# Key-value and row products of four tiles in quarters of the array, 64 by 64

## The chip, the core and the metric

One core of one Trainium2 chip. The metric is the time of the whole kernel on the device, in microseconds. The engines are named as the profile names them: PE (TensorE, matmuls; its weight loads are the row PEld), DVE (VectorE), ACT (ScalarE), POOL (GpSimd) and SP (SyncE, which here issues DMAs).

## What is computed

Attention without a softmax on 8 batches, 8 heads, 576 rows and 64 columns, each head's output divided by the root of its mean square, and a two-layer network behind it:

```python
kv  = einsum('bhsd,bhse->bhde', k, v)          # 64 x 64 for each head
out = einsum('bhsd,bhde->bhse', q, kv)
x   = out / sqrt(mean(out * out, -1) + 1e-6) * g_norm    # -> 4608 rows x 512
h   = x @ w_in                                  # 512 -> 2048
y   = (h / (1 + exp(-1.702 * h))) @ w_out       # 2048 -> 512
```

Inputs and result are float32; the matmuls take float16 and add up in float32.

## The kernel before

There are nine tiles, t = 0 to 8. Tiles 0 to 7 hold the first 512 rows of one batch each, tile 8 the last 64 rows of all eight. While PE runs the network of tile t, the attention of batch b = t + 1 is made in between, and the key-value product of batch t + 2. The order is written by hand: each engine executes its instructions in the order in which the program issues them, and two dictionaries, `u1` for the first layer and `u2` for the second, say after which step a piece of other work is issued. `at2(i, f)` puts `f` behind matmul i of the second layer.

From tile 1 on each layer is done with seven half-size products instead of eight (a scheme with sums of quarters). In the first layer (`SevenIn`, `hid_seven`) the steps stand in a plan such as `LATER`, two digits for a group of columns and a product; the matmuls are those of L589. In the second layer (`Seven.run`) the products come in the order 1, 5, 6, 2, 7, 3, 4 with 16 matmuls each (L709, 128 x 256), so matmuls 0 to 15 are product 1, 16 to 31 product 5, 80 to 95 product 3. Products 5, 6, 7 and 3 take sums of the gated rows, the quarters 0 to 3 of `gS`, which VectorE forms (L641); `later` in the plan says when. In `LATER` the first half of quarter 3 is formed behind matmul 58, and two products of the first layer's last group ('34') are left for matmul 15.

PSUM has eight banks: three with the tag `att` (pool `ps_a`), three `hT` (`ps_h`), two `o` (`ps_o`). The tiles of a pool take its banks in turn, so a new tile waits for the readers of the third last one.

The attention of a batch b from 2 on, as far as the change touches it:

- `kv_products` (L264): for four pairs of heads, 5 x 2 matmuls (L248) with 128 rows of `k` as weights (64 columns, one head) and 64 columns of `v`. One head of the pair goes to the upper half of the PSUM partitions, the other to the lower. The fifth step is the rest, 64 rows, the other 64 being zero. All goes to one bank, `kvp`.
- `kv_copies` (L271, `keep_kv`): four copies of 64 x 256 from `kvp` to `kb` (the tile `kvd`), since each head's product is wanted on the upper and on the lower 64 partitions. On ScalarE, behind matmul 52.
- `rows` (L328): 2 x 16 matmuls (L337) with 64 rows of the transposed queries as weights (128 columns) and 64 columns of `kb`. The two row halves of the array (`half`) write to two banks.
- Then `squares` of the four banks on ScalarE (L347, `sq`), `add_up` on VectorE (L353, `sum`), `roots` on ScalarE (L362), `turn` on VectorE (L367, `x`), and a DMA that transposes `x` into `xT`, the input of the next tile. `xS` (L517) are sums of quarters of `xT`.

In `LATER`, `rows` is `(15, 15)`: behind matmul 15 of the second layer PE runs the key-value products of batch t + 2, and straight after them the rows of batch b.

Of the kernel before, what the change touches and what calls it, by code (L numbers as in the profile page):

```python
# [8 lines left out]
F32 = mybir.dt.float32  # L9
# [3 lines left out]
P = 128  # L13
# [3 lines left out]
def kernel(  # L17
# [203 lines left out]
    class Attention:  # L221
# [47 lines left out]
        def kv_products(self):  # L269
            self.kvp = ps_a.tile([P, NPAIR, D], F32, name="kvp", tag="att")  # L270
            for js in (range(J), (J,)):  # L271
                for c in range(NPAIR):
                    self.kv_product(self.kvp[:, c, :], c, js, c == 0)

        def kv_copies(self, engine):
            self.engine = engine
            self.keep_kv(0, NPAIR)
# [35 lines left out]
        def out(self, c):  # L313
# [11 lines left out]
            nc.scalar.activation(sq[:, 0:n], t, AFT.Square)  # L325
            self.o[c] = (t, sq, n)

        def rows(self, i):  # L328

            t = [  # L330
                pool.tile([P, DM], F32, name="outR", tag=tag)
                for pool, tag in ROW_BANKS[i]
            ]
            for h in range(H):
                for half in range(2):
                    r = slice(half * D, (half + 1) * D)
                    nc.tensor.matmul(  # L337
                        t[half][:, h * D : (h + 1) * D],
                        self.qTd[r, h * (J // 2) + i, :],
                        self.kb[r, h // 2, half, 1 - h % 2, :],  # L340
                        start=(h == 0),
                        stop=True,
                        skip_group_check=True,
                    )
            for half in range(2):
                sq = attn.tile([P, SM], F16, name="sq", tag="sq", bufs=4)
                nc.scalar.activation(sq, t[half], AFT.Square)  # L347
                self.o[2 * i + half] = (t[half], sq)
# [572 lines left out]
    for fo in COLS[0:GROUP]:  # L921
# [38 lines left out]
        "aahh",  # L960
        {15: '34'},
        (0, 0, 6, 11),
        {'rows': (15, 15), 'add_up': (17, 20, 24, 28), 'table': 24, 'roots': (28, 29), 'turn': (35, 38, 46, 48)},
    )
    LAST_TWO = Plan(
# [21 lines left out]
    for t in range(NT):  # L987
# [6 lines left out]
        def at2(i, f, *args):  # L994
            u2.setdefault(i, []).append(lambda: f(*args))  # L995
# [40 lines left out]
        elif b < B:  # L1036
            todo = plan(t)
            at = todo.attn
            if t == 1:
                at1(todo.steps.index("kv"), of(b, "kv_all", "D"))  # L1040
                at1(5, start, b)
                at1(5, of(b, "transpose_q", kv_rows["v"][0:1, RS + H * D - 1 : RS + H * D]))
                at1(5, of(b, "transpose_rest"))
                at1(5, store_early, 0, 0, SM // 2)
                at1(4, nc.scalar.preload_act_table_set, "gelu_apprx_sigmoid_and_others")
                for n, i in ((1, 8), (2, 11)):
                    at1(i, weight_sum, n, 4, HF)
# [73 lines left out]
```

## Time and profile before

| | |
|---|---|
| median of 3 runs | 258.75 us (258.61 to 259.12) |
| the profiled execution | 258.24 us, its span 256.5 us |
| busy: PE, DVE, ACT, POOL | 98%, 76%, 69%, 23% of the span |
| granted clock of TensorE | full in every slice |
| L248, key-value products | 240 matmuls with 128 rows, 197 ns mean |
| L337, rows | 192 matmuls, 191 ns mean |

A matmul's duration is its way through the array; many are under way at once, so PE's time is read from the distance between starts. In the chain of work that ended last, PE has nearly all of the span: the two layers (L709 and L589) 38% each, `kvp` 2%, `outR` 1%. "Idle before" is the time in which an engine stood still ahead of an instruction, with the one that ended it.

### The profile page before, as it was taken

The numbers are of one execution on the slowest core, as the hardware profiler recorded it, in microseconds if no ns is written. First come the engines' busy times: TensorE is split into PE (matmuls) and PEld (weight loads), VectorE is DVE, ScalarE is ACT, GpSimd is POOL, SyncE is SP. The second block draws the span as 40 slices with busy tenths as digits, with TensorE's granted clock in tenths as the row PEclk, the third lists the DMA queues.
The fourth block names the chain that finished last, engine by engine and source line by source line (L and its number), as shares of the span: only waits on it lengthen the run. The fifth ranks groups of instructions, "written<-read, shape, count | busy, mean of one in ns | idle before, by whom it ended". The sixth has DMA issues, their size and how long they took to land.

```text
span 256.5 us, 6359 instructions
## 1 busy us (share of the span) xinstructions
PE 250.5 (98%) x2600; PEld 203.8 (79%) x2600; DVE 194.4 (76%) x341; ACT 177.0 (69%) x322; POOL 57.8 (23%) x94
## 2 busy tenths in 40 slices
PE   7899999999999999999999999999999999999994
PEld 2444544788888888888888888888888889888883
DVE  1557585999958895989588867986899687857872
ACT  3469725978759885989598958995798569537800
POOL 8882155404080104301340143000000000000013
PEclk9999999999999999999999999999999999999999
DMA  7999999998999989998999699909500730012005
GB/s 180 189 201 205 205 204 196 191 178 128 165 183 214 118 115 172 216 273 109 211 170 137 87 228 128 177 4 156 184 4 0 93 155 3 0 75 91 3 19 146
DMA packets 68703, 35.33 MB, mean 138 GB/s; under 512 B 37986, under 2 KB 66274, under 8 KB 68418
## 3 DMA queue, kind: packets, MB, share of 16 engines
q0 software_dynamic: 37648, 18.31, 55.4%
q1 hardware_dynamic: 30624, 16.29, 28.7%
q8 instruction: 20, 0.33, 0.6%
q10 hardware_dynamic: 402, 0.33, 0.4%
q14 instruction: 9, 0.07, 0.1%
HBM read 36.70 MB, written 9.44 MB: 180 GB/s over the span
## 4 chain that ended last, share of the span: by engine, by line
PE 94%; DMA 2%; POOL 2%; DVE 0%; issue 0%
PE o L709 38%; PE h L589 38%; PE o L822 5%; PE hT L478 5%; DMA vbuf<-in_v_dram 2%; PE kvp L248 2%; PE outR L337 1%; PE ss L384 1%; POOL qraw L91 1%; PE outT L307 1%; POOL kraw L91 0%; PE q L459 0%; PE kvp L261 0%; PE idle L869 0%; PE kv L261 0%; PE outT L311 0%
## 5 line engine op out<-in xcount | busy, mean ns | idle before, releaser
L566 ACT ACTIVATE gT<-h 128x512 f16<-128x512 f32 x96 | 52.4, 602 | 5.7 <-PE h L589 5.7
L589 PEld LDWEIGHTS <-ws 128*128 128x128 f16 x512 | 50.0, 98 | 6.0
L709 PEld LDWEIGHTS <-gS 128*128 128x128 f16 x512 | 49.0, 98 | 6.2 <-DVE gS L641 0.3
L589 PE MATMUL h<-xS,ws 128*128 128x256 f16 x384 | 52.2, 273 | 0.0
L709 PE MATMUL o<-tw,gS 128*128 128x256 f16 x384 | 45.6, 273 | 0.0
L589 PEld LDWEIGHTS <-w_in_sb 128*128 128x128 f16 x384 | 37.5, 98 | 4.7
L709 PEld LDWEIGHTS <-gT 128*128 128x128 f16 x384 | 37.6, 98 | 4.3
L709 PE MATMUL o<-w_out_sb,gT 128*128 128x256 f16 x256 | 31.4, 273 | 0.0
L589 PE MATMUL h<-xT,w_in_sb 128*128 128x256 f16 x224 | 31.1, 272 | 0.0
L603 DVE TENSOR_TENSOR h<-h,s 128x512 f32<-128x512 f32 x32 | 22.3, 698 | 4.4 <-PE h L589 2.8
L605 DVE TENSOR_TENSOR s<-h,s 128x512 f32<-128x512 f32 x32 | 22.1, 691 | 4.3 <-PE h L589 3.5
L686 DVE TENSOR_TENSOR osb<-o,qf 128x512 f32<-128x512 f32 (+1 forms) x25 | 16.7, 668 | 11.2 <-PE o L709 11.1
L743 POOL DMA_DIRECT2D out_dram<-osb x6 | 3.2, 538 | 93.2 <-DVE osb L686 93.2
L641 DVE TENSOR_TENSOR gS<-gT 128x512 f16<-128x512 f16 (+2 forms) x32 | 21.3, 684 | 0.6 <-ACT gT L566 0.6
L566 ACT ACTIVATE gT<-s 128x512 f16<-128x512 f32 x32 | 19.8, 628 | 2.8 <-DVE s L605 2.8
L589 PE MATMUL h<-xS,w_in_sb 128*128 128x256 f16 x128 | 18.9, 273 | 0.0
L353 DVE TENSOR_REDUCE sum<-sq 128x8 f32<-128x512 f16 x24 | 14.9, 679 | 4.7 <-ACT sq L347 4.7
L995 ACT ACT_TABLE_LOAD x14 | 18.0, 1283 | 0.3
L535 DVE COPY s<-h 128x512 f32<-128x512 f32 x19 | 13.0, 685 | 6.5 <-PE h L589 6.4
L325 ACT ACTIVATE sq<-outT 128x512 f16<-128x512 f32 (+1 forms) x16 | 7.8, 493 | 14.3 <-PE outT L307 8.7
L115 POOL DMA_DIRECT2D kraw<-in_k_dram x7 | 6.0, 855 | 49.1 <-PE kvp L248 32.5
L386 ACT ACTIVATE rs<-ss,eps_t 128x512 f32<-128x512 f32 (+1 forms) x16 | 9.2, 581 | 11.2 <-PE ss L384 11.2
(105 smaller groups left out, 372.2 us busy)
## 6 DMA issues: line engine op xcount, KB each, us to landing
out_dram<-osb SPq DMA_DIRECT2D x8, 512.0 KB, 5.4
kraw<-in_k_dram POOLq DMA_DIRECT2D x5, 512.0 KB, 6.0
vbuf<-in_v_dram POOLq DMA_DIRECT2D x5, 512.0 KB, 10.0
out_dram<-osb SPq DMA_DIRECT2D x2, 1024.0 KB, 4.1
qraw<-in_q_dram POOLq DMA_DIRECT2D x3, 512.0 KB, 11.0
qbuf<-in_q_dram POOLq DMA_DIRECT2D x3, 512.0 KB, 12.8
out_dram<-osb SPq DMA_DIRECT2D x6, 192.0 KB, 6.7
w_in_sb<-in_moe_w_in_dram POOLq DMA_DIRECT2D x2, 512.0 KB, 9.6
```

The source lines that it names most:

```text
L353: nc.vector.tensor_reduce(out=self.sum4[:, j, :], in_=self.o[j][1].rearrange("p (x d) -> p x d", d=D), op=ALU.add, axis=mybir.AxisListType.X,)
L478: nc.tensor.matmul(self.h[fo], w_in_sb[:, ko, fo * P : (fo + 1) * P], self.x[:, ko], start=(ko == 0), stop=(ko == KO - 1),)
L535: (nc.vector.tensor_copy if engine == "D" else nc.scalar.copy)(to, src)
L566: nc.scalar.activation(self.gT[:, to, n * TH : (n + 1) * TH], src, AFT.Gelu_apprx_sigmoid)
L589: nc.tensor.matmul(bank[name][:, a], w, x, start=(p in (1, 5) and a == 0 and k == 0), stop=(k == KH - 1), skip_group_check=True,)
L603: nc.vector.tensor_add(bank["z"], bank["x"], self.s5)
L605: nc.vector.tensor_add(self.s5, bank["x"], self.s5)
L641: op(s[:, n, lo], a, b)
L686: nc.vector.tensor_add(o, ps, self.kept[with_][:, m])
L709: nc.tensor.matmul(o, a, w, start=(p in (1, 2, 5) and i == 0 and (mo == 0 or split)), stop=(i == HF - 1), skip_group_check=True,)
L822: nc.tensor.matmul(os[mo], gT[:, fo, mo * P : (mo + 1) * P], w_out_sb[:, fo, :], start=(fo == 0), stop=(fo == FO - 1),)
L995: u2.setdefault(i, []).append(lambda: f(*args))
```

## The change

For t = 2 to 5 (the third to the sixth tile) both blocks are made of matmuls that use a quarter of the array, 64 rows by 64 columns. The key-value product of 128 rows is split in two of 64, whose sums go to two banks `kvh`. ScalarE copies the second bank to SBUF (`kvl`, 128 x 256, float32), and VectorE adds it to the first while it writes `kb`, in two instructions of 64 x 256. The other two of the four blocks of `kb` are then copied from SBUF to SBUF by ScalarE behind matmul 52 (`spread`). The rest now uses the upper 64 rows of the array only. In a row product the 128 columns of queries are split in two. In the plan `LATER`, `rows` is (16, 16); the seventh tile (t = 6) uses this plan too, with the row products as before.

```diff
+        def kv_quarters(self):
+            self.kvh = [ps_a.tile([P, NPAIR, D], F32, name="kvh", tag="att") for _ in range(2)]
+            for c in range(NPAIR):
+                for j in range(J + 1):
+                    for hl in range(2):
+                        h = 2 * c + hl
+                        x = RS + h * D if j == J else h * RW + j * D
+                        for half in range(1 if j == J else 2):
+                            r = slice(half * D, (half + 1) * D)
+                            nc.tensor.matmul(
+                                self.kvh[half][hl * D : (hl + 1) * D, c, :],
+                                kv_rows["k"][r, x : x + D],
+                                kv_rows["v"][r, x : x + D],
+                                start=(j == 0 and c == 0),
+                                skip_group_check=True,
+                                stop=(j == J - half),
+                            )
+
+        def add_halves(self):
+            lower = attn.tile([P, NPAIR, D], F32, name="kvl", tag="kvl", bufs=1)
+            nc.scalar.copy(lower, self.kvh[1])
+            for hl in range(2):
+                r = slice(hl * D, (hl + 1) * D)
+                nc.vector.tensor_add(self.kb[r, :, hl, 1 - hl], self.kvh[0][r], lower[r])
+
+        def spread(self):
+            for hl in range(2):
+                r, to = (slice(x * D, (x + 1) * D) for x in (hl, 1 - hl))
+                nc.scalar.copy(self.kb[to, :, 1 - hl, 1 - hl], self.kb[r, :, hl, 1 - hl])
...
+        def rows_quarters(self, i):
...
+            for h in range(H):
+                for m in range(2):
+                    to = slice(m * D, (m + 1) * D)
+                    for half in range(2):
+                        r = slice(half * D, (half + 1) * D)
+                        nc.tensor.matmul(
+                            t[half][to, h * D : (h + 1) * D],
+                            self.qTd[r, h * (J // 2) + i, to],
+                            self.kb[r, h // 2, half, 1 - h % 2, :],
...
-        {'rows': (15, 15), 'add_up': (17, 20, 24, 28), 'table': 24, 'roots': (28, 29), 'turn': (35, 38, 46, 48)},
+        {'rows': (16, 16), 'add_up': (17, 20, 24, 28), 'table': 24, 'roots': (28, 29), 'turn': (35, 38, 46, 48)},
...
-                at2(at["rows"][0], of(t + 2, "kv_products"))
-                at2(52, of(t + 2, "kv_copies", "A"))
+                at2(at["rows"][0], of(t + 2, "kv_quarters"))
+                at2(at["rows"][0], of(t + 2, "add_halves"))
+                at2(52, of(t + 2, "spread"))
...
-                    at2(at["rows"][j], of(b, "rows", j))
+                    at2(at["rows"][j], of(b, "rows_quarters" if 1 < t < B - 2 else "rows", j))
```

On PE, in the third tile, before: the last matmul that is left of the first layer, the key-value products and the rows, and the first matmul of product 5 (a line of "..." stands for equal pairs).

```order
L589 MATMUL h_1273<-xS,w_in_sb 128x256
L248 LDWEIGHTS kraw
L248 MATMUL kvp<-vbuf,kraw 64x64
...
L337 LDWEIGHTS qTd
L337 MATMUL outR<-kvd_90,qTd 128x64
...
L709 LDWEIGHTS gS
L709 MATMUL o_1349<-tw,gS 128x256
```

And now, with the line numbers of the changed file (L642 is L589, L762 is L709, L284 and L368 are the new products):

```order
L642 MATMUL h_1273<-xS,w_in_sb 128x256
L762 LDWEIGHTS gS
L762 MATMUL o_1349<-tw,gS 128x256
L284 LDWEIGHTS kraw
L284 MATMUL kvh<-vbuf,kraw 64x64
...
L368 LDWEIGHTS qTd
L368 MATMUL outR<-kvd_90,qTd 64x64
...
L762 LDWEIGHTS gS
```

There are now 72 key-value matmuls where 40 stood and 64 of rows where 32 stood; the sizes are those of the output. The first matmul of product 5 has moved ahead of them.

On ScalarE at the same place, from the copy of product 1's bank on, before:

```order
L535 COPY qf<-o_1350 128x512
L566 ACTIVATE gT<-h_1273 128x2x256
L347 ACTIVATE sq<-outR 128x512 x4
L995 ACT_TABLE_LOAD
L362 ACTIVATE sum_1466<-sum_1466,eps_t 128x16 x2
L535 COPY qf<-o_1349 128x512
L535 COPY qf<-o_1350 128x512
L535 CAST kvd_89<-kvp 64x4x64 x4
```

And now:

```order
L588 COPY qf<-o_1350 128x512
L619 ACTIVATE gT<-h_1273 128x2x256
L295 COPY kvl<-kvh 128x256
L400 ACTIVATE sq<-outR 128x512 x4
L1048 ACT_TABLE_LOAD
L415 ACTIVATE sum_1535<-sum_1535,eps_t 128x16 x2
L588 COPY qf<-o_1349 128x512
L588 COPY qf<-o_1350 128x512
L303 COPY kvd_89<-kvd_89 64x4x64 x2
```

A copy of one half stands ahead of the squares, and two copies stand where four casts stood. On VectorE, from the sum of `gS` behind matmul 16 on, now:

```order
L694 TENSOR_TENSOR gS<-gS,gT 128x1024
L298 TENSOR_TENSOR kvd_89<-kvh,kvl 64x4x64 x2
L406 TENSOR_REDUCE sum_1535<-sq 128x8 x4
L694 TENSOR_TENSOR gS<-gT,gS 128x1024
L420 TENSOR_TENSOR x_1563<-outR,sum_1535 128x512 x4
L694 TENSOR_TENSOR gS<-gT,gS 128x1024
L739 TENSOR_TENSOR osb<-o_1581,qf 128x2x256
```

Only the second of these lines is new; the last sum of `gS` is the first half of quarter 3.

More of the change, by code (lines that the diff above doesn't have):

```diff
@@ L326, in out @@
             self.o[c] = (t, sq, n)
+        def rows_quarters(self, i):
+            t = [
+                pool.tile([P, DM], F32, name="outR", tag=tag)
+                for pool, tag in ROW_BANKS[i]
+            ]
+            for h in range(H):
[7 more added lines that the diff above has]
+                            self.kb[r, h // 2, half, 1 - h % 2, :],
+                            start=(h == 0),
+                            stop=True,
+                            skip_group_check=True,
+                        )
+            self.squares(i, t)
         def rows(self, i):
@@ L344, in rows, with squares @@
                     )
+            self.squares(i, t)
+        def squares(self, i, t):
             for half in range(2):
```

## The prediction

> **What bounds the kernel now.** I read the page first (engines, chain), then the timeline of the third tile, then the groups by form, then narrow windows of the timeline where a spacing is needed.
>
> ```profile
> span 256.5 us, 6359 instructions
> PE 250.5 (98%) x2600; PEld 203.8 (79%) x2600; DVE 194.4 (76%) x341; ACT 177.0 (69%) x322; POOL 57.8 (23%) x94
> PE 94%; DMA 2%; POOL 2%; DVE 0%; issue 0%
> ```
>
> TensorE (PE) is busy for 98% of the span and makes 94% of the chain that ended last. A change counts only by the time that it adds to or takes from PE's own stream, or by a wait that it puts there. In the third tile (t = 2) that stream reads:
>
> ```profile
> 87.17 0.60 PE L589 MATMUL h<-xS,w_in_sb 128*128 128x256 f16 x4
> 87.69 0.82 PE L248 MATMUL kvp<-vbuf,kraw 128*64 128x64 f16 x40
> 88.45 0.64 PE L337 MATMUL outR<-kvd,qTd 64*128 64x64 f16 x32
> 89.02 3.67 PE L709 MATMUL o<-tw,gS 128*128 128x256 f16 x32
> ```
>
> The columns are start, length to the last end, then the operation. To turn lengths into starts one needs the duration of one instruction, from the groups by form:
>
> ```profile
> L709 PE MATMUL o<-tw,gS 128*128 128x256 f16 x384 | 45.6, 273 | 0.0
> L248 PE MATMUL kvp<-vbuf,kraw 128*64 128x64 f16 x240 | 4.9, 197 | 0.0
> L337 PE MATMUL outR<-kvd,qTd 64*128 64x64 f16 x192 | 3.8, 191 | 0.0
> L248 PEld LDWEIGHTS <-kraw 128*64 128x64 f16 x240 | 4.3, 112 | 1.3 <-issue 1.3
> L337 PEld LDWEIGHTS <-qTd 64*128 64x128 f16 x192 | 3.1, 95 | 0.6 <-issue 0.4
> ```
>
> - Ordinary step: the 32 L709 matmuls start 31 steps apart in 3.67 - 0.27 = 3.40 us, 0.11 each.
> - Way in: the last L589 starts at 87.17 + 0.60 - 0.27 = 87.50, the first key-value product at 87.69: 0.19, of which 0.08 is more than a step.
> - Key-value block: first to last start 0.82 - 0.20 = 0.62 us for 40 matmuls.
> - Between the blocks: 88.45 - (87.69 + 0.62) = 0.14.
> - Rows: 0.64 - 0.19 = 0.45 us for 32.
> - Way out: 89.02 - 88.90 = 0.12.
>
> From 87.50 to 89.02 that is 1.52 us. Each change of the array's form (128*128 to 128*64, to 64*128, and back) costs some 0.08 to 0.11 us beyond a normal spacing. How the small matmuls are spaced is seen in three windows that end a slot later each:
>
> ```profile
> 87.69 0.28 PE L248 MATMUL kvp<-vbuf,kraw 128*64 128x64 f16 x6
> 87.69 0.32 PE L248 MATMUL kvp<-vbuf,kraw 128*64 128x64 f16 x8
> 87.69 0.35 PE L248 MATMUL kvp<-vbuf,kraw 128*64 128x64 f16 x10
> 88.44 0.11 PEld L337 LDWEIGHTS <-qTd 64*128 64x128 f16 x4
> ```
>
> Each further 0.03 us holds two more: one for each half of the array, started together. So there are 20 slots of two (0.62/19 = 0.033 us) in the key-value block, and 16 (0.45/15 = 0.030) in the rows. The fourth line shows four weight loads of 0.095 us each, two for each row half, that all begin within 0.11 - 0.095 = 0.015 us.
>
> **The change part by part.** *PE.* Key-value: per pair of heads 16 matmuls on the 512 rows and 2 on the rest, so 72 instead of 40. If four 64 by 64 quarters start together, that is 4 x 4 slots of four and 4 of two (the rest uses one row half): again 20 slots. Rows: 64 instead of 32, by four again 16 slots. Nothing is saved in the slots; what goes is the change of form between the blocks, 0.14 - 0.03 = 0.11 us. Against that, the rows' weights are now 64 columns, as the key-value ones are: I take their slot at 0.033, not 0.030, so 15 x 0.003 = 0.05 more. Ways in and out stay (0.19, 0.12). Net: -0.11 + 0.05 = -0.06 us a tile, four tiles. Ends: if all slots went at the rows' pace, -0.11 - 19 x 0.003 = -0.17; if only two of the four quarters ever run together, there are 36 and 32 slots instead of 20 and 16, 16 x 0.033 + 16 x 0.030 = +1.01, less 0.11: +0.90 us a tile. I take the near end, because pairs already start together on halves in both directions, and weight loads of two row halves do too.
>
> [...]
>
> One `o` matmul moves ahead of the block (rows at 16 instead of 15), which moves the block by 0.11 and PE's work by nothing. The bank that it opens was last read by a gate that stands ahead of the copy at 87.36 in the rows below, so it does not wait. The halves hold two of the three `att` banks, so the rows' fourth bank is now the one that the late gate reads until 88.45; it is written from about 87.80 + 0.62 + 0.03 + 0.27 = 88.72. The load of the next keys, which GpSimd issues when the block is done with them, comes 0.11 later.
>
> *ScalarE and VectorE.* The copy of one half and two additions stand ahead of the squares and their sums:
>
> ```profile
> 87.36 0.59 ACT L535 COPY qf<-o 128x512 f32<-128x512 f32 x1 [0.39 <-PE o L709]
> 87.85 0.60 ACT L566 ACTIVATE gT<-h 128x512 f16<-128x512 f32 x1
> 88.89 2.06 ACT L347 ACTIVATE sq<-outR 128x512 f16<-128x512 f32 x4 [0.44 <-PE outR L337]
> 92.27 0.51 ACT L362 ACTIVATE sum<-sum,eps_t 128x16 f32<-128x16 f32 x2
> 87.81 0.69 DVE L641 TENSOR_TENSOR gS<-gS,gT 128x1024 f16<-128x1024 f16 x1
> 89.52 2.46 DVE L353 TENSOR_REDUCE sum<-sq 128x8 f32<-128x512 f16 x4 [1.01 <-ACT sq L347]
> 91.90 0.68 DVE L641 TENSOR_TENSOR gS<-gT,gS 128x1024 f16<-128x1024 f16 x1
> 92.61 2.48 DVE L367 TENSOR_TENSOR x<-outR,sum 128x512 f16<-128x512 f32 x4
> 95.01 0.68 DVE L641 TENSOR_TENSOR gS<-gT,gS 128x1024 f16<-128x1024 f16 x1
> L325 ACT ACTIVATE sq<-outT 128x256 f16<-128x256 f32 x8 | 3.1, 392 | 5.5 <-PE outT L311 5.5
> L535 DVE CAST kvd<-kvp 64x256 f16<-64x256 f32 x4 | 1.7, 419 | 0.0
> L535 ACT CAST kvd<-kvp 64x256 f16<-64x256 f32 x20 | 7.3, 367 | 0.7 <-PE kvp L248 0.5
> ```
>
> ScalarE is idle for 0.44 us before the squares and VectorE for 1.01 before the sums; both holes are filled. Worked out: the block starts at 87.69 + 0.11 = 87.80, the second half's last matmul a slot before the end at 88.39, done 0.20 later, copy from about 88.63 (0.04 for the signal: the rows' first bank is done at 88.85, the squares start at 88.89). The copy, nearest the 128x256 row, 0.39: 89.02. Two additions, nearest the 64x256 row: 0.42 each, or 0.34 if they overlap as the four sums do (2.46 for four of 0.68 is 0.59 apart, 0.08 of overlap). With 0.03 for the signal they end the hole at 89.73 to 89.89, so the sums start 0.21 to 0.37 later than 89.52. ScalarE itself runs up to 0.13 later. At 92.61 VectorE waited for ScalarE's first root (free at about 91.90 + 0.60 = 92.50), so 0.11 is swallowed there: the `x` products and the `gS` sum behind them come 0.13 to 0.26 later. The four casts at 52 become two copies, ScalarE has 2 x 0.37 less to do there; nobody waits for it.
>
> Who waits for that `gS` sum (row quarter 3) is product 3 of the second layer, at once after product 7:
>
> ```profile
> 95.80 0.21 PEld L709 LDWEIGHTS <-gS 128*128 128x128 f16 x2
> 96.02 0.27 PE L709 MATMUL o<-w_out_sb,gS 128*128 128x256 f16 x1
> 68.90 0.68 DVE L641 TENSOR_TENSOR gS<-gT,gS 128x1024 f16<-128x1024 f16 x1
> 69.64 0.10 PEld L709 LDWEIGHTS <-gS 128*128 128x128 f16 x1
> 69.27 0.71 PE L709 MATMUL o<-w_out_sb,gS 128*128 128x256 f16 x5
> ```
>
> The sum ends at 95.69, the matmul starts at 96.02. In the tile before, it ended at 69.58, its weight load began at 69.64, and the five matmuls from 69.27 still kept 0.11 apart ((0.71 - 0.27)/4), so the matmul was at 69.71: 0.13 after the sum's end is in time. The slack is 0.33 - 0.13 = 0.20, and 0.14 once PE is 0.06 earlier. A shift of 0.13 to 0.26 against it: a wait of 0 to 0.12 us. I take 0.04. Net for a tile: -0.06 + 0.04 = -0.02.
>
> Two more slacks shrink and hold:
>
> ```profile
> 99.13 0.42 DVE L517 TENSOR_TENSOR xS<-xT 128x512 f16<-128x512 f16 x1
> 99.74 1.92 PE L589 MATMUL h<-xT,w_in_sb 128*128 128x256 f16 x16
> 100.48 0.70 POOL L120 DMA_DIRECT2D vbuf<-in_v_dram x1
> 113.82 0.82 PE L248 MATMUL kvp<-vbuf,kraw 128*64 128x64 f16 x40
> DMA to landing us min/median/max: 9.3/10.1/13.0
> ```
>
> The transposed `x` is there at 99.13 at the latest, PE reads it at 99.74: 0.26 fits. The rest of the keys and values is now read in the fifth slot instead of after 16 of 20, 0.36 us earlier in the block; issued at 100.48 with at most 13.0 to landing it is there at 113.5, and the read moves from some 114.3 to 114.1.
>
> **Sum.** 4 x -0.02 = -0.1 us. The profiled execution took 258.24 us (span 256.5 and 1.7 around it), 0.5 less than the median of the runs, 258.75; I put the difference on the median: 258.65, with its own ends 4 x -0.17 = -0.7 (258.05) and 4 x (-0.06 + 0.12) = +0.2 (259.0). A difference of 0.2% (0.52 us) is about what a measurement of this kernel can tell from no change.
>
> **Rivals.** *The quarters do not run four at a time* (slower). For it: every slot shown holds two, and eight instructions must now be issued in 0.033 us where four are. Against it: the four weight loads within 0.015 us. Price: at the full +0.90, 4 x 0.90 = +3.6 (262.35); half way, slots of 0.045, 36 x 0.012 - 0.11 = +0.32 a tile, +1.3 (260.05). It passes 0.2% when a slot is over 0.040 ((0.13 + 0.11)/36 on 0.033). Chance 0.23, the full price 0.08.
>
> [...]
>
> *VectorE's chain ends last* (slower): copy and additions dearer than the rows suggest (0.69 as a 128x512 addition takes, instead of 0.42) would put the `gS` sum another 0.5 us later, a shift of 0.7 in all against the slack of 0.14: -0.06 + 0.56 = +0.50 a tile, +2.0 (260.65); at half of that +1.0 (259.65). It passes 0.2% from a shift of 0.33. Chance 0.13.
>
> *All goes at the rows' pace and nothing waits* (faster): -0.17 a tile, 258.05. For it: no matmul form here shows why four should be slower than two. Against: the key-value slot is the longer one. Chance 0.17.
>
> That the forms are not what the change says is excluded by the order: both are 64x64 there.
>
> **Chances and range.** Forecast 0.47 (within 0.2%), faster 0.17, slower 0.23 + 0.13 = 0.36. Range 257.9 to 260.5: it holds the forecast, the faster case, and the slower ones up to their half prices; left out are the full price of the first rival and the upper part of the second, some 0.15. The forecast's own range is 258.05 to 259.0.
>
> **What would show it.** In the changed trace: the two blocks together 0.62 + 0.03 + 0.50 us from first to last start, four matmuls to each 0.033; a spacing of 0.03 between them instead of 0.14; the sums starting at +0.2 to +0.4; the first matmul of product 3 with a gap of at most 0.12 us behind the `gS` sum. The forecast is wrong if a block of rows is longer than 0.6 us, or if PE's idle time at product 3 is over 0.2 us a tile.

## The result, and the profile after

| | before | changed |
|---|---|---|
| median of the runs | 258.67 us (258.01 to 259.18, 7 runs) | 260.18 us (259.30 to 260.73, 7 runs) |
| ratio, 95% interval | | 1.0053 (1.0031 to 1.0074) |
| profiled execution (span) | 258.24 us (256.5) | 260.41 us (258.6) |

The kernel became slower by 1.5 us. The forecast was 258.65 us with "no change" as the likeliest; the time lies inside the range, on the slower side. The page of the changed kernel, engines and chain:

```profile
span 258.6 us, 6875 instructions
PE 252.0 (97%) x2856; PEld 204.2 (79%) x2856; DVE 197.0 (76%) x349; ACT 175.9 (68%) x318; POOL 58.0 (22%) x94
PE 86%; DMA 7%; POOL 4%; issue 1%; DVE 0%
```

PE's share of the chain fell from 94 to 86%, DMA's rose from 2 to 7%: PE now waits for something that it didn't wait for. The waits of PE, summed by what ended them, name it (the same view of before has no line for `kvp` or `kvh`):

```profile
engine line waited for: us in total, times, longest us
...
PE kvp L248 <- DMA vbuf<-in_v_dram: 1.1, 1, 1.1
```

It stands in the second tile, in a block that the change doesn't touch: the last eight key-value products, those of the leftover 64 rows, wait for their values.

```profile
70.53 0.69 PE L248 MATMUL kvp<-vbuf,kraw 128*64 128x64 f16 x32
72.32 0.32 PE L248 MATMUL kvp<-vbuf,kraw 128*64 128x64 f16 x8 [1.10 <-DMA vbuf<-in_v_dram]
```

The third tile, where the prediction was worked out, on PE, ScalarE and VectorE:

```profile
88.64 0.60 PE L642 MATMUL h<-xS,w_in_sb 128*128 128x256 f16 x4
89.08 0.27 PE L762 MATMUL o<-tw,gS 128*128 128x256 f16 x1
89.28 0.79 PE L284 MATMUL kvh<-vbuf,kraw 64*64 64x64 f16 x70
89.88 0.23 PE L368 MATMUL outR<-kvd,qTd 64*64 64x64 f16 x2
89.90 0.20 PE L284 MATMUL kvh<-vbuf,kraw 64*64 64x64 f16 x2
89.93 0.76 PE L368 MATMUL outR<-kvd,qTd 64*64 64x64 f16 x62
90.62 3.56 PE L762 MATMUL o<-tw,gS 128*128 128x256 f16 x31
...
97.66 0.28 PE L762 MATMUL o<-w_out_sb,gS 128*128 128x256 f16 x1
...
90.13 0.37 ACT L295 COPY kvl<-kvh 128x256 f32<-128x256 f32 x1 [0.20 <-PE kvh L284]
90.46 2.06 ACT L400 ACTIVATE sq<-outR 128x512 f16<-128x512 f32 x4
...
93.83 0.51 ACT L415 ACTIVATE sum<-sum,eps_t 128x16 f32<-128x16 f32 x2
...
90.53 0.86 DVE L298 TENSOR_TENSOR kvd<-kvh,kvl 64x256 f16<-64x256 f32 x2 [0.55 <-ACT kvl L295]
91.42 2.46 DVE L406 TENSOR_REDUCE sum<-sq 128x8 f32<-128x512 f16 x4
93.80 0.68 DVE L694 TENSOR_TENSOR gS<-gT,gS 128x1024 f16<-128x1024 f16 x1
94.52 2.48 DVE L420 TENSOR_TENSOR x<-outR,sum 128x512 f16<-128x512 f32 x4
96.92 0.68 DVE L694 TENSOR_TENSOR gS<-gT,gS 128x1024 f16<-128x1024 f16 x1
```

From the last 128 x 256 matmul ahead of the blocks (89.08) to the next one (90.62) it is 1.54 us, where 1.52 stood. Product 3 starts at 97.66, behind the sum's end at 97.60; at its usual distance it would have started 0.15 earlier.

Laid beside each other start by start, every matmul of the two networks against its counterpart, the traces differ by 2.16 us at the last matmul: 0.20 at the program's start, 1.29 at the second tile's leftover rows, and in each of the four tiles 0.01 (in one 0.03) at the blocks and 0.13 to 0.16 at product 3: 0.65 in all; 0.02 is left. So 0.65 us recur tile by tile; 1.29 came once, and the before's profile was 0.4 us under its own median. The 0.65 alone would give 259.3, the lowest of the seven runs.

### The profile page after: what moved, and what is told of

Its sections match the earlier page's. It is cut to its first block, busy times and chain, and to the rows that moved or that the text cites. A ratio compares the mean times of both kernels' runs of the same rounds, so it can differ in the third digit from the quotient of the medians.

```text
span 258.6 us, 6875 instructions
## 1 busy us (share of the span) xinstructions
PE 252.0 (97%) x2856; PEld 204.2 (79%) x2856; DVE 197.0 (76%) x349; ACT 175.9 (68%) x318; POOL 58.0 (22%) x94
## 4 chain that ended last, share of the span: by engine, by line
PE 86%; DMA 7%; POOL 4%; issue 1%; DVE 0%
PE h L642 37%; PE o L762 35%; PE o L875 5%; DMA vbuf<-in_v_dram 5%; PE hT L531 4%; DMA w_in_sb<-in_moe_w_in_dram 3%; PE kvh L284 1%; PE outR L368 1%; POOL qraw L91 1%; POOL kraw L91 1%; POOL vbuf L91 1%; PE ss L437 1%; POOL w_in_sb L180 1%; PE kvp L248 0%; PE q L512 0%
## 5 line engine op out<-in xcount | busy, mean ns | idle before, releaser
L642 PEld LDWEIGHTS <-ws 128*128 128x128 f16 x512 | 50.1, 98 | 5.9
L762 PEld LDWEIGHTS <-gS 128*128 128x128 f16 x512 | 49.1, 98 | 7.1 <-DVE gS L694 1.3
L642 PE MATMUL h<-xS,ws 128*128 128x256 f16 x384 | 52.2, 273 | 0.0
L762 PE MATMUL o<-tw,gS 128*128 128x256 f16 x384 | 46.4, 273 | 0.0
L642 PEld LDWEIGHTS <-w_in_sb 128*128 128x128 f16 x384 | 37.5, 98 | 4.7
L762 PEld LDWEIGHTS <-gT 128*128 128x128 f16 x384 | 37.6, 98 | 4.3
L762 PE MATMUL o<-w_out_sb,gT 128*128 128x256 f16 x256 | 31.4, 273 | 0.0
L642 PE MATMUL h<-xT,w_in_sb 128*128 128x256 f16 x224 | 31.1, 272 | 0.0
L642 PE MATMUL h<-xS,w_in_sb 128*128 128x256 f16 x128 | 18.9, 273 | 0.0
L588 ACT COPY h<-h 128x512 f32<-128x512 f32 x27 | 15.4, 577 | 2.1 <-PE h L642 1.8
L642 PE MATMUL h<-xT,ws 128*128 128x256 f16 x112 | 16.8, 272 | 0.0
```

The costliest lines, as they stand in the source:

```text
L588: (nc.vector.tensor_copy if engine == "D" else nc.scalar.copy)(to, src)
L642: nc.tensor.matmul(bank[name][:, a], w, x, start=(p in (1, 5) and a == 0 and k == 0), stop=(k == KH - 1), skip_group_check=True,)
L762: nc.tensor.matmul(o, a, w, start=(p in (1, 2, 5) and i == 0 and (mo == 0 or split)), stop=(i == HF - 1), skip_group_check=True,)
```

## Experiments

Two things had to be explained: the regular 0.16 us a tile, and about 0.85 us by which the median exceeds it. Below, "extra" is what such a comparison with the profile of before shows at one place. Tiles are counted from one, so the change is in the third to the sixth; a block means the key-value and row products of a tile.

### One part at a time

**The gate sum earlier.** The changed kernel with the last `gS` sum ahead of the fourth `x` product:

```diff
-        {0: ((0, 8, 2),), 16: ((4, 8, 1),), 29: ((4, 8, 3),), 58: ((0, 4, 3),)},
+        {0: ((0, 8, 2),), 16: ((4, 8, 1),), 29: ((4, 8, 3),), 47: ((0, 4, 3),)},
```

> The changed kernel, with the first half of the gS quarter 3 formed ahead of the last x product (47 instead of 58 in LATER). Theory A (VectorE's additions push that sum past the start of product 3, a wait of 0.14 us in each of four tiles): the gap of 0.25 us at product 3 goes back to 0.11, the time falls by 0.5 to 0.6 us against the changed kernel, to about +0.9 over the kernel before. Rival B (the cost sits elsewhere: in the load of the keys and values that the second tile waits for): the gap goes, but the time stays within 0.2 us of the changed kernel, since a later wait takes it.

261.45 us (261.19 to 261.86), ratio 1.0109 (1.0089 to 1.013). The wait at product 3 is gone, as it should; the blocks still cost 0.01. In the third tile the sum now ends at 95.71, 0.51 us ahead of product 3 (VectorE's sum, then PE):

```profile
95.03 0.68 DVE L694 TENSOR_TENSOR gS<-gT,gS 128x1024 f16<-128x1024 f16 x1
...
96.22 0.27 PE L762 MATMUL o<-w_out_sb,gS 128*128 128x256 f16 x1
```

But the fourth tile's block stops for 1.40 us and the sixth's for 1.34, and 0.37 is lost in the seventh tile, which uses the same plan. The edit cured one wait and showed that there are others which no theory so far had.

**Key-value quarters only** (the rows in halves again):

```diff
-                    at2(at["rows"][j], of(b, "rows_quarters" if 1 < t < B - 2 else "rows", j))
+                    at2(at["rows"][j], of(b, "rows", j))
```

> The changed kernel with the rows as before (two by two, 64 rows by 128 columns). Theory A (a key-value slot of four quarters costs what a slot of two halves did, 0.032 us, and it is the row quarters that are slower, 0.038 a slot): key-value block 0.63 us, a change of form of 0.13, rows 0.45, so the blocks take as long as before within 0.02 us; the additions still make product 3 wait 0.14 us. Over the kernel before: +0.5 us plus what the second tile waits. Rival B (quarters cost the same in both blocks): the block is 0.1 us a tile longer than in the changed kernel.

260.34 us (259.76 to 260.52), 1.0067 (1.0046 to 1.0089). Blocks 0.01 faster than before, wait at product 3 0.16 (in three of the four tiles), and 0.86 us extra in the fourth tile's block, in two pieces.

**Row quarters only** (the kernel before with this line, key-value products and copies as they were):

```diff
-                    at2(at["rows"][j], of(b, "rows", j))
+                    at2(at["rows"][j], of(b, "rows_quarters" if 1 < t < B - 2 else "rows", j))
```

> The kernel before with only the rows of the four tiles in quarters (rows at 15, key-value products in halves, copied by ScalarE at 52). Theory A: rows 0.60 us instead of 0.45 with the change of form ahead of them kept, +0.12 to +0.15 us a tile, no wait at product 3: +0.5 to +0.6 us over the kernel before. Rival B (quarters are as quick as halves when they don't follow quarters): rows 0.50, +0.2 us in all, within what can be told.

259.95 us (259.54 to 261.59), 1.006 (1.0037 to 1.0082). No wait at product 3, blocks 0.09 slower each, and in the fourth tile 1.32 extra. The timeline of the third tile and the stop in the fourth:

```profile
88.00 0.82 PE L248 MATMUL kvp<-vbuf,kraw 128*64 128x64 f16 x40
88.75 0.74 PE L368 MATMUL outR<-kvd,qTd 64*64 64x64 f16 x64
89.42 1.81 PE L762 MATMUL o<-tw,gS 128*128 128x256 f16 x15
...
116.04 0.32 PE L248 MATMUL kvp<-vbuf,kraw 128*64 128x64 f16 x8 [1.13 <-DMA vbuf<-in_v_dram]
```

The change of form between the blocks is 88.75 - 88.00 - 0.62 = 0.13 here, and the 64 quarters take 0.74 - 0.19 = 0.55 from first to last start, against 0.45 for the 32 halves: 9 ns from start to start instead of 15. Counted by four, a slot is 0.55/15 = 0.037, not 0.033.

**Memory moved, nothing else.** The kernel before with the tile `kvl` (1 KB for each partition) allotted where the change has it, one element written:

```diff
+                if t == 2:
+                    at2(60, lambda: nc.vector.memset(
+                        attn.tile([P, NPAIR, D], F32, name="kvl", tag="kvl", bufs=1)[0:1, 0, 0:1], 0.0))
```

> The kernel before with the 1 KB tile kvl allotted as in the changed kernel (one element of it is written once), so that the tiles behind it in SBUF lie where they lie there; no other instruction differs. Theory A (the 0.9 us that the four tiles don't explain are not a matter of addresses): same time as the kernel before within 0.3 us. Rival B (the DMAs of the second tile are slower at the new addresses): +0.7 to +1.0 us, with PE waiting about 1.3 us for the key-value products of the second tile.

258.57 us (258.25 to 258.96), 0.9997 (0.9986 to 1.0007); no extra anywhere but 0.25 at the start. The addresses are not it.

### What the irregular stops are

Two kinds can be told apart by the place in PE's stream. Some stand ahead of the first product of the leftover rows, and the releaser is the landing of `vbuf`. Others stand in the middle of the rows or behind them, where the program has no wait: in the second run above,

```profile
115.33 0.58 PE L387 MATMUL outR<-kvd,qTd 64*128 64x64 f16 x27
116.24 0.26 PE L387 MATMUL outR<-kvd,qTd 64*128 64x64 f16 x5 [0.34 <-issue]
```

"issue" says that PE had nothing to wait for. If one counts PE's recorded instructions (matmuls, weight loads, and the eleven waits and drains among them) from the start, this stop stands at number 2497, and the sixth tile's with the earlier sum at 4033. Both are 63 short of a multiple of 256 (10 x 256, 16 x 256); that 63 instructions of the stream are not recorded is an inference from this. The page of the changed kernel has a queue of its own for instructions, with 22 packets of 16 KB where before has 20. PE's recorded matmuls and weight loads rose by 512, from 5200 to 5712, so one packet stands for 256 of them:

```profile
q8 instruction: 22, 0.36, 0.6%
```

So theory A was: a block of quarters issues 272 instructions in some 1.2 us where halves issued 144 in the same time; if a block of instructions ends inside it and the next one was fetched late, PE has none left. Theory B: the stops are landings and waits alone. To move the ends without touching anything else, instructions were added to the idle products in the first 6 us:

```diff
-    busy(12)
+    def short(n):
+        for _ in range(n):
+            nc.tensor.matmul(
+                idle_ps[:, 0:D], kvb[1][:, 0, :], kvb[1][:, 0, 0:D], start=True, stop=True
+            )
+
+    busy(10)
+    short(19)
```

> The changed kernel with 34 more TensorE instructions in its first 6 us (two of the twelve idle 128x512 products give way to nineteen idle 128x64 products, which take about the same time); everything behind is the same work in the same order. Theory A (instruction blocks): TensorE's instructions are fetched 256 at a time; a fetch that starts late, beside other transfers, leaves TensorE without instructions when 256 of them go by in a block of quarters (272 instructions in 1.25 us), and a fetch that falls among the DMA transposes of the normalised attention output holds these up by 1.3 us, so that the next values are asked for later. The shift puts the block ends 63 to 177 instructions behind the start of each of the four attention blocks, so that no two fall into one block. Left is the change's own cost, 0.16 us a tile: 258.65 + 0.65 = 259.3 us, runs within 259.0 to 259.7. Theory B (the landing of keys and values varies by itself, or quarters are slow for another reason): as the changed kernel, 260.2 us, runs from 259.3 to 260.7.

260.86 us (259.21 to 260.92), 1.0076 (1.0049 to 1.0102): not what A said. There is no stop at a block end within the blocks (at number 1985, 46 instructions behind the third tile's block, PE loses 0.2), but the fourth tile's leftover rows wait longer than in any other run:

```profile
114.47 0.32 PE L284 MATMUL kvh<-vbuf,kraw 64*64 64x64 f16 x16
116.21 0.63 PE L284 MATMUL kvh<-vbuf,kraw 64*64 64x64 f16 x53 [1.42 <-DMA vbuf<-in_v_dram]
```

The same with `busy(6)` and `short(83)`, so that ends fall into the blocks:

> The same with 154 more TensorE instructions (six idle 128x512 products give way to eighty-three idle 128x64 ones, about 2.3 us of each). Theory A: block ends fall 57 and 19 instructions ahead of the attention blocks of the third and fourth tile and so again inside them, 199 and 237 instructions in: TensorE stops there for want of instructions, 0.5 to 1.5 us at each of two or three tiles, at the instruction whose number is 256 times a whole number less 63: 260.5 to 263 us. Theory B: 260.2 us as the changed kernel.

263.34 us (261.62 to 265.53), 1.0192 (1.0134 to 1.0249). PE stops 2.39 us in the fourth tile at number 2753 = 11 x 256 - 63, 1.01 in the fifth at 3521 = 14 x 256 - 63 and 0.28 in the sixth at 4289 = 17 x 256 - 63:

```profile
116.70 0.59 PE L368 MATMUL outR<-kvd,qTd 64*64 64x64 f16 x44
119.49 0.34 PE L368 MATMUL outR<-kvd,qTd 64*64 64x64 f16 x18 [2.20 <-issue]
119.77 1.46 PE L762 MATMUL o<-tw,gS 128*128 128x256 f16 x6
```

Two windows behind the first stop (length, then busy time and count of PE, PEld, DVE, ACT and POOL, then the granted clock):

```profile
119.40:121.40 2.00, 1.91 (x26) 1.43 (x27) 0.97 (x3) 1.51 (x3) 0.00 (x0) 0.60 1.16 106
121.40:123.40 2.00, 2.00 (x12) 1.44 (x10) 1.77 (x4) 1.58 (x4) 0.00 (x0) 0.55 1.18 164
```

These are means over windows that lie partly outside the slow stretch: over 119.77 to 123.17 alone it is 0.50. So the granted clock was 0.50 for 3.4 us; by an estimate from these two numbers (3.4 x 0.5) that cost another 1.7 us. The control is the kernel before with the same 154 instructions:

> The kernel before with 154 more TensorE instructions at the start, those of the run that stopped 2.39 us in the fourth tile. Its attention blocks issue 144 instructions, not 272, so that 256 never go by in one. Theory A: no stop at any block end; the start's own cost is 0.2 to 1.5 us (1.2 us by the shifted changed kernel's first tile): 258.8 to 260.1 us. Theory B (a shift by itself makes stops in any form): 261.5 to 263 us.

259.29 us (258.79 to 260.35), 1.0035 (1.0022 to 1.0048). In its profile 0.50 us is the start's own cost; no block end shows a stop. Once more the leftover rows wait, 0.26 in the fourth tile (the block from 114.31 takes 1.02 to the rows instead of 0.75). So the shift alone makes no such stop: A, not B.

The stops at block ends that the profiles have inside or just behind an attention block, with the fetch ahead of them from the records of DMA packets (us; the last four kernels are described below):

```
kernel                       block end   fetch             PE goes on   later than the fetch's end
changed                      16 x 256    166.84 to 167.81  169.16       1.35   (stop 0.08)
changed, second profile      16 x 256    167.19 to 168.07  169.47       1.40   (0.77)
earlier sum                  16 x 256    167.75 to 168.72  170.12       1.40   (1.39)
key-value quarters only      10 x 256    112.56 to 114.81  116.24       1.43   (0.53)
154 more                     11 x 256    117.10 to 118.08  119.49       1.41   (2.39)
154 more                     14 x 256    145.87 to 147.00  148.58       1.57   (1.01)
154 more                     17 x 256    174.36 to 175.56  176.98       1.42   (0.28)
34 more                       8 x 256     89.83 to  90.79   92.18       1.39   (0.30)
leftover last                16 x 256    165.91 to 166.88  168.24       1.36   (0.20)
leftover last, sum earlier   16 x 256    166.29 to 167.23  168.51       1.28   (0.63)
the same and 34 more          8 x 256     89.06 to  90.43   92.03       1.60   (0.27)
and leftover keys earlier     8 x 256     90.25 to  91.62   93.14       1.52   (0.39)
```

The distances between starts are in brackets; some 0.01 to 0.11 of them is normal. PE goes on 1.28 to 1.60 us behind the end of the packet each time, whatever the stop's length: it is the fetch that it waits for. Over the 368 block ends of the 18 profiles that have a fetch (matched in order), no instruction behind an end started sooner than 1.28 us after the end of its fetch; in the five profiles without quarters the least is 3.9 us, so nothing waits for a fetch there. The releaser in the profile is wrong at these stops (in the second profile it names ScalarE's copy, done half a microsecond before).

### The leftover rows

The changed kernel needs them 0.13 us into the block, pair by pair; before they came last, 0.50 in. Put last again:

```diff
-            for c in range(NPAIR):
-                for j in range(J + 1):
-                    for hl in range(2):
...
+            for js in (range(J), (J,)):
+                for c in range(NPAIR):
+                    for j in js:
+                        for hl in range(2):
```

> The changed kernel with one edit: the leftover rows of keys and values (53 of 309 positions) are multiplied behind all others of the tile, as in the kernel before, and not pair by pair; block ends and everything else as in the changed kernel. Theory A (late leftover rows and block ends are two causes of stops): the leftover rows are needed 0.43 us later, so that the fourth tile's wait for them goes or shrinks, and the block itself loses its 0.01 us and gains 0.02 against the kernel before, as the combined run showed: 258.65 + 4 x (0.15 - 0.02) = 259.2 us, with some runs at 259.5 to 260 from the block end in the sixth tile and the second tile's landing. Theory B (block ends alone make the stops): 259.9 to 260.2 us.

(The leftover is 64 of 576 positions; the text gives other numbers.) 259.52 us (259.31 to 259.89), 1.004 (1.0026 to 1.0053): 0.7 less than the changed kernel, or 0.5 when the median of before in the same round is taken from each. No wait for the leftover rows; 0.18 at the block end 16 x 256; product 3 waits 0.09 to 0.10; and the blocks are 0.018 us a tile faster than before, not 0.01 slower. Third tile:

```profile
88.46 0.77 PE L285 MATMUL kvh<-vbuf,kraw 64*64 64x64 f16 x68
...
89.11 0.74 PE L369 MATMUL outR<-kvd,qTd 64*64 64x64 f16 x61
89.78 3.56 PE L763 MATMUL o<-tw,gS 128*128 128x256 f16 x31
```

61 rows in 0.74 - 0.19 = 0.55 us, where the changed kernel has 62 in 0.76 - 0.19 = 0.57. So the order alone makes this difference. Why is not shown.

The reverse edit in the kernel before, the leftover rows pair by pair (`for c in range(NPAIR): self.kv_product(self.kvp[:, c, :], c, range(J + 1), c == 0)`):

> The kernel before with one edit: the leftover rows are multiplied pair by pair with the others, and so are needed 0.13 us into the block instead of 0.50 us, in every tile from the second. Theory A (the need comes before the landing): the fourth tile waits for them in part of the runs, 0 to 1 us: 258.8 to 259.4 us. Theory B (the wait has to do with quarters, not with the order): 258.6 us.

258.53 us (258.25 to 259.00), 0.9998 (0.9989 to 1.0007). No wait; theory A of this run fell. The order alone is not enough: the landing has to be late too. The last of the 16 parts of the leftover values came 1.82 us ahead of the fourth tile's block in this profile, 0.29 ahead in before, 0.95 ahead with 30 more instructions (below), and 0.72 behind the block's start with 154 more. In ten of the thirteen profiles with any quarters PE waited for it, until 0.4 to 1.8 us behind the block's start; with row quarters only it did so although the leftover rows come last there. The spread is wide: in the changed kernel's first profile they landed 5.1 us ahead of the block, in its second (below) 0.6 behind its start. Part of this may have a reason, in the rows of SyncE and GpSimd: the `x` transposes (a DMA) of the third tile, and the instruction with which GpSimd waits for them before it asks for the values, in before

```profile
93.92 2.64 SPq L373 DMA_TRANSPOSE xT<-x  x2
...
98.70 0.18 POOL L127 COPY mark<-xT 1x1 f16<-1x1 f16 x1 [9.12 <-DMA xT<-x]
```

and with key-value quarters only:

```profile
94.51 2.64 SPq L426 DMA_TRANSPOSE xT<-x  x2
...
100.47 0.18 POOL L127 COPY mark<-xT 1x1 f16<-1x1 f16 x1 [10.51 <-DMA xT<-x]
```

4.78 us against 5.96. Over all 18 profiles and three tiles each, the transposes took 4.70 to 5.19 us in the 25 cases in which no instruction fetch (of PE or of another engine) began 0.3 to 4.5 us behind their start, and 5.30 to 6.27 in the 29 in which one did (these two bounds were not set beforehand). More PE instructions move the fetches, here one to 97.8 us, among the transposes. An attempt to do this to the kernel before failed: 30 more instructions at its start,

> The kernel before with 30 more TensorE instructions at the start (two idle 128x512 products give way to seventeen 128x64 ones). Theory A: the fetch that came at 99.1 us, behind the third tile's transposes, now comes at about 97.4 us, among them: they land 1.2 to 1.4 us later (6.1 us behind their first issue instead of 4.8), the next values are asked for so much later, and the fourth tile's attention block waits 0.3 to 1.3 us for the leftover values: 258.9 to 259.9 us. Theory B: no difference, 258.6 us.

258.73 us (258.00 to 259.37), 1.0008 (0.9993 to 1.0022). The fetch came at 98.5 us, when the transposes had just landed (4.77 us), so nothing was tried by it. That a fetch holds the transposes up is therefore a coincidence in 54 cases, not shown by an edit; and why the landing came late in the run with 34 more instructions (asked for as early as in before, 1.7 us behind the block's start) stays open.

### Mending all of it

> The changed kernel with three edits: the 34 more instructions at the start, the gate sum of the last quarter made eleven turns earlier (which took away the wait at product 3 in the run with the earlier sum), and the 53 leftover rows of keys and values multiplied behind all others of the tile, as in the kernel before, instead of pair by pair. Theory A: wait at product 3 gone (-0.15 us a tile), no stop at an instruction block's end, and 0.43 us more time for the leftover rows' landing: 258.65 + 4 x 0.01 = 258.7 us. Theory B: as the run with the earlier sum, 261.0 to 261.5 us.

259.22 us (258.91 to 260.13), 1.0031 (1.0018 to 1.0045), 2.2 less than the earlier sum alone. No stop at a block end; 0.28 at the fourth tile's leftover rows; 0.37 in the seventh tile, where the earlier sum delays an `x` product that PE waits for (the same in the first run), and 0.4 at the start. Then with the earlier sum in the four tiles only, without and with the 34 instructions:

> The changed kernel with the leftover rows last and the gate sum of the last quarter eleven turns earlier in the four halved tiles only; the instruction blocks end where those of the changed kernel end. Theory A: no wait at product 3; in the sixth tile TensorE crosses a block end (instruction 16 x 256 - 63) 210 instructions into its attention block, as in the run with the earlier sum, where it stopped 1.39 us: 258.6 + up to 1.4 = 259.0 to 260.0 us. Theory B (block ends do not matter, only loads and sums do): 258.6 us.

> The same with the 34 more TensorE instructions at the start, so that the block ends lie 63, 101, 139 and 177 instructions into the four attention blocks. Theory A: no stop is left but a few tenths for the fourth tile's leftover rows: 258.65 - 4 x 0.02 + 0.1 to 0.3 = 258.6 to 258.9 us, no slower than the kernel before. Theory B: 258.6 us, as without the shift.

260.58 us (259.61 to 260.93), 1.0073 (1.0054 to 1.0092), and 259.24 us (258.61 to 259.83), 1.0021 (1.0006 to 1.0036). Both are above what theory A gave. The two kernels differ by where instruction blocks end, and their medians by 1.3 us. The profiled runs (259.61, the fastest of its six, and 259.41) do not show all of that: 0.2. In the profile without the 34 PE waits 0.42 us for the fourth tile's leftover rows and stops in the sixth tile, 0.63 from start to start at 16 x 256:

```profile
168.52 0.44 PE L369 MATMUL outR<-kvd,qTd 64*64 64x64 f16 x31 [0.44 <-ACT kvl L296]
```

With them it doesn't stop there; what is lost is 0.17 at 8 x 256 behind the third tile's block, and 0.81 at the fourth tile's leftover rows:

```profile
115.64 0.22 PE L285 MATMUL kvh<-vbuf,kraw 64*64 64x64 f16 x3 [0.62 <-DMA vbuf<-in_v_dram]
```

Two more were to show which of the remaining losses matters: leftover rows last and 34 instructions, with the sum where the change has it, and the last kernel with the leftover keys asked for ahead of the transposes, so that the leftover values are asked for 0.68 us earlier (`for n in main if rest else ""` in the loads).

> The changed kernel with the leftover rows (64 of 576 positions) last and the 34 more TensorE instructions at the start; the gate sum stays where the change has it. Theory A (three causes: block ends, leftover rows needed early, wait at product 3): only the wait at product 3 is left, 0.09 us a tile, against 0.02 gained in the block: 258.6 + 4 x 0.07 + 0 to 0.2 for the start = 258.9 to 259.1 us. Theory B (the two edits each only move a stop elsewhere): 259.5 to 260.2 us.

> The kernel with the leftover rows last, the earlier gate sum and the shift of 34, and one edit more: the leftover rows of the keys are asked for with the other keys, before the transposes, and not between the values and their leftover rows, so that the latter are asked for 0.68 us earlier. Theory A: the fourth tile's wait, 0.8 us in the last such profile, shrinks by 0.5 to 0.8: 258.6 to 258.9 us. Theory B (the landing is set by how the stores share the DMA, whenever it is asked for): as without this edit, 259.2 us.

259.25 us (258.53 to 260.67), 1.0026 (1.0008 to 1.0043), and 258.98 us (258.28 to 259.69), 1.0015 (1.0003 to 1.0027). In the second profile nothing waits in the fourth tile; 0.29 is a stop just behind the third tile's block, at 8 x 256 - 63, and the start took 1.2 us longer than in before. In the first the start took 1.7 us longer, and the leftover rows of the fourth tile 0.30. Neither is faster than before. The best that the profiles allow, 0.018 us a tile, can't be measured.

### The changed kernel once more

> The changed kernel itself once more. Theory A (a fixed cost of 0.16 us in each of the four tiles, and stops that come and go): the fixed part again within 0.02 us a tile; of the stops, up to 1.6 us at the fourth tile's leftover rows, up to 1.4 us at the block end in the sixth tile, or the second tile's landing; the lowest run at 259.2 to 259.4 us, most at 259.9 to 260.8. Theory B (the second tile's stop of 1.29 us is the change's own): it is there again, and the fourth and sixth tile have none.

260.21 us (260.01 to 260.63), 1.006 (1.0046 to 1.0074). The second tile has no stop; the fourth and the sixth have:

```profile
114.71 0.32 PE L284 MATMUL kvh<-vbuf,kraw 64*64 64x64 f16 x16
115.34 0.63 PE L284 MATMUL kvh<-vbuf,kraw 64*64 64x64 f16 x53 [0.32 <-DMA vbuf<-in_v_dram]
...
168.43 0.48 PE L368 MATMUL outR<-kvd,qTd 64*64 64x64 f16 x31
169.47 0.44 PE L368 MATMUL outR<-kvd,qTd 64*64 64x64 f16 x31 [0.55 <-ACT kvl L295]
```

0.50 at the leftover rows, 0.71 at the block end, and again 0.01 and 0.14 in each of the third to fifth tiles. That is theory A: a fixed part, and stops that come at different places.

## Why the prediction was wrong, point by point

The forecast put the blocks and the wait at product 3 at -0.02 us a tile and every other wait at nothing. Two terms of the sum were too small, and together they cost 0.16 us a tile; a slack said to hold and a wait that the prediction does not have make stops of about 0.9 us.

- **Four quarters at a time**: right, and with it the first rival fell. 72 key-value matmuls start within 0.63 us (70 of them in 0.79 - 0.19 = 0.60, 9 ns each, against 0.62/39 = 16 ns in halves), as worked out. From 89.28 on, windows of the changed trace that end at 89.29, 89.32, 89.35 and 89.38 hold 4, 8, 12 and 16 of them.
- **The rows' slot**: mis-sized. The term was +0.05 us a tile (0.033 a slot); alone behind halves the rows cost +0.10 (0.037), and in the changed kernel +0.17 (0.62 instead of 0.45, 0.041 a slot). The change of form between the blocks did go, as forecast: the rows begin 0.02 us ahead of the last key-value products, 0.16 sooner than before. The blocks came out at +0.01, not -0.06, in four tiles 0.3 us. "A block of rows longer than 0.6 us" was named as what would make the forecast wrong; the rows' own 64 starts take 90.62 - 0.12 - 89.88 = 0.62.
- **The wait at product 3**: right in kind, 0.15 instead of 0.04, over its upper end of 0.12; 0.45 us more in four tiles. Copy and additions came when they were worked out to, the sums at +0.42 (91.42 - 89.28 + 0.11 - (89.52 - 87.69)), a little over the 0.37. The step that failed is the 0.11 that was to be "swallowed" at VectorE's wait for the root. In before the root and the `gS` sum ahead of the `x` products end together (92.58), so that trace can't tell which of them the products waited for. In the changed trace the first root is done by 94.14, and yet the products start at 94.52, 0.72 behind the sum's start as before (0.71): there was no wait to swallow anything, and the whole shift, 0.43, reached the last `gS` sum. The slack was larger than the 0.20 of the prediction: product 3 started 0.06 behind the sum's end here, not 0.13, so 0.33 - 0.06 = 0.27, and 0.43 - 0.27 is the wait within 0.01. This is the second rival's wait without its condition (copy and additions were no dearer than worked out), at 0.6 us instead of its 1.0 to 2.0.
- **Slacks said to hold**: the fourth bank and `xT` did. That of the leftover rows did not. The read moved as worked out, 0.37 us earlier in the block. What failed is "at most 13.0" from issue to landing, which came from one profile: it was 8.0 us in the changed kernel's first profile, 13.7 in its second, and 15.0 with 34 more instructions. With the leftover rows last the median is 0.5 to 0.7 us lower, of which 0.3 is block and product 3.
- **Not in the prediction at all**: that PE's instructions come in blocks of 256 through the DMA (two packets more for 512 more of them), and that nearly twice as many of them in the same time (272 in some 1.2 us, 144 before) can outrun the fetch (stops of up to 2.39 us). The wait was put at nothing without a reason. Moving the ends alone changed the median by 1.3 us in one pair (259.24 and 260.58) and by 3.1 in another (260.18 and 263.34; the profile of the latter, its slowest run, has 1.2 us more at the start and 1.7 of slow clock in it). In two other pairs the ratios to before can't be told apart: 1.0053 and 1.0076, 1.0040 and 1.0026.
- **Slips in the sums**: the second rival's prices are added to 258.65, the first's to 258.75; on one footing they are 260.75 and 259.75. A slot of 0.045 is called half way, but half of +0.90 a tile would be +1.8 in all, not +1.3. Neither moves the forecast.

The sum for the median: 258.65, 4 x 0.16 = 0.65, and about 0.9 us that is put down to stops, since the two profiles of the changed kernel show nothing else: in one 1.29 at the second tile, in the other 0.50 and 0.71. (In the second the sixth tile has no wait at product 3 behind its stop.) The runs that have no profile may divide it otherwise. The second tile's is in unchanged code and came in one of 18 profiles; whether the change made it is not settled.

## What to carry to other kernels

Splitting matmuls to fill the array costs instructions: count how many PE issues in the densest stretch (272 in some 1.2 us here), and where the 256-instruction blocks end there (up to 2.4 us were lost at one end), before trusting slots. A stop on PE with the releaser "issue", or with one that ended long before, is looked up by its instruction number and the instruction queue's packets. A slack against a DMA landing that comes from one profile is a sample, not a bound (the leftover values took 13.0 us in before, 8.0 and 13.7 in the two profiles of the changed kernel, 15.0 with 34 more instructions): with the read of late data left at the end of the block the median was 0.5 to 0.7 us lower here.

## What was not expected of the hardware

- A fetch is one packet of 16 KB for 256 PE instructions (20 packets in before, 22 with 512 instructions more); it took 0.9 to 1.6 us (once 1.98, once 2.25), and where PE had stopped it went on 1.3 to 1.6 us behind its end. At the stops it had begun up to 2.7 us behind the execution of the block end ahead of it (number 3777 ran at 165.1 us with the earlier sum, the fetch began at 167.75). With 272 instructions in some 1.2 us up to 2.4 us were lost at one end; with 144, in the five profiles without quarters, nothing was lost at one, and PE never went on sooner than 3.9 us behind a fetch's end.
- A stop of 2.4 us was followed by a granted clock of 0.50 for 3.4 us, and the mean of that execution is 0.992; in the other 17 profiles, whose stops in the blocks were at most 1.6 us, it is 0.997 or more.
- DMA transposes that took 4.7 to 5.2 us took 5.3 to 6.3 where an instruction fetch began among them (25 and 29 cases; no edit tried it).
- The weight load of a 64 x 64 quarter of the rows took 105 ns, of a 64 x 128 half 95; the slot grew from 0.030 to 0.037 us with row quarters only.
